# Sums over experts moved to DRAM, and two sets of second-matrix operands, in an attention and mixture kernel

## The chip, the cores and the metric

The kernel runs on one core of a Trainium2 chip. The metric is the device time of one execution in microseconds (us). TensorE (PE in the profile) multiplies matrices, VectorE (DVE) and ScalarE (ACT) do the elementwise work, and SyncE (SP) issues nearly all DMA transfers, in the order of its instruction stream. Each engine executes its own stream in order and waits on semaphores for the others.

## The reference, cut to what matters

Linear attention feeds a dense network with 2048 hidden features, and its output feeds a mixture of eight experts whose weights come from a balanced table P. All products and sums are float32 in the reference.

```python
N, D, E, F = (2304, 512, 8, 1024)
...
P = np.exp(logits)
for _ in range(8):
    P /= P.sum(1, keepdims=True) + 1e-09
    P /= P.sum(0, keepdims=True) + 1e-09
    P *= N / E
out = np.zeros((N, D), dtype=np.float32)
for e in range(E):
    h = np.maximum(x @ w1[e], 0.0)
    ye = h @ w2[e]
    out += P[:, e:e + 1] * ye
```

## The kernel before

The dense network is treated as two layers `e` = 0 and 1 (`M` = 2), the experts as `e` = 2 to 9 (`NL` = 10). The 2304 rows are 18 tiles of 128, and they are worked in three parts `p` of six tiles. Each float32 operand is stored as a pair of float16 numbers (`halves`, line 379: one ACT cast and one DVE subtraction), and each product is three float16 matmuls (`hi_lo_mms`, line 390). The products of an expert use a scheme of seven instead of eight half-size products; the index `m_` runs over these seven.

For each expert and part there are four units of the class `Quad` (line 1068: first matrix, 7 x 6 matmuls of 384 columns each, results split into the hidden operands `hop`) and then three units of the class `Outs` (line 1250: second matrix, 7 x 4 x 3 matmuls of 256 columns each). So an expert has 12 Quads with 504 matmuls of 384 columns, and 9 Outs with 756 of 256 columns. At most three units are in flight (`flight`, line 1003), four have buffers (`unit_bufs`), and eight banks of PSUM are shared (`banks`). A unit gives its place in `flight` back in `give`, after its products `c21` and `c12` have been read out of PSUM. Of an Outs, `take` (line 1296) reads `c11`, `c12` or `c22` out of PSUM with one DVE addition, hands the bank on in `after`, and only then calls `add_to`, which adds the scaled block to the sum over experts. `take_c21` calls `add_to` on the PSUM block itself and hands the bank on after it.

The sums over experts, `acc` (line 988), are 18 tiles of 2 KB a partition in SBUF at the region `BR`. They stay there from the first expert to the last; the attention and the dense network used the region before (`ys`, line 407). An Outs changes two tiles, in four blocks of 256 columns.

The weights of an expert come in four parts of 1 MB (`st_load`, line 853): parts 0 and 1 are the first matrix, parts 2 and 3 the second. They pass through three staging slots of 8 KB a partition (`st_view`, line 839), in the order of the number `4 * e + part`; a part is loaded when the part three numbers earlier has been consumed (`st_guard`, line 843). DVE takes the largest absolute value of a part (`st_max`, line 868), `w_prep` (line 883) makes a scale from both parts of a matrix, and `w1_split` (line 918) and `w2_split` (line 958) scale the part and write the float16 pairs into `W1` and `W2`. There is one set of each. A product's operand of expert `e` is written after the last matmul of expert `e - 1` on it (`w1_used`, `w2_used`). So the first matrix is split while the last part's Outs of the expert before run, and the second while the first part's Quads of its own expert run. With three slots, part 3 of an expert takes the slot of its part 0, and so is loaded only when half of that expert's first matrix has been split.

The order of all instructions on each engine is written by a planner (`Sched`, line 96): a list scheduler with estimated costs, run several times, that takes what can start first and, of that, what is due first by the latest starts of the run before. DMA issues are planned on SP the same way, with a cost by size (`dma`, line 336). The inputs of a part, `X`, are 2.7 MB and come back from DRAM by `x_load` (line 746) for most parts.

## Time and profile before

| | |
|---|---|
| median of 3 runs | 1834.15 us (1829.84 to 1835.17) |
| time of the profiled execution | 1839.03 us |
| its span, first to last instruction | 1837.2 us |
| mean granted TensorE clock | 0.986 |
| PE / PEld busy | 97% / 70% |
| DVE / ACT busy | 83% / 59% |
| DMA traffic | 129.09 MB, 70 GB/s |

Busy shares are over the span. "Idle before" in the groups names what ended an engine's wait. A window row gives, for a stretch of the span, each engine's busy time and number of instructions, then the granted clock (1.00 is 2.4 GHz and 0.50 is 1.2 GHz), the mean busy share of the DMA engines and what they moved in GB/s.

### The profile page before, as it was taken

Reading aid. Unit: us, or ns where it says so; the run is one execution under the profiler, and the core shown is the slowest. Engines: PE = TensorE matmul, PEld = TensorE weight load, DVE = VectorE, ACT = ScalarE, POOL = GpSimd, SP = SyncE. Lnnn points to the kernel's source line nnn. Section 1 sums busy time; section 2 is a strip of 40 time slices with the busy share of each in tenths; the row PEclk is TensorE's granted clock in tenths of the full one; section 3 lists DMA queues with packets and bytes.
Section 4 is the critical chain, followed back from the end, with each engine's and each line's share of the span. In section 5 each row is a group of like instructions: output and inputs, shape, how many; then the busy total and the mean of one; then the engine's idle time right before and its main releaser. Section 6 shows DMA issues by size and latency. Waiting matters only on the chain.

```text
span 1837.2 us, 31972 instructions
## 1 busy us (share of the span) xinstructions
PE 1773.4 (97%) x12898; PEld 1277.2 (70%) x12898; DVE 1523.3 (83%) x3294; ACT 1086.8 (59%) x2284; POOL 2.8 (0%) x11
## 2 busy tenths in 40 slices
PE   4989999999999999999999999999999999999999
PEld 3855666666677767776777777677767777776777
DVE  5789976779887999699779869985998799789866
ACT  4757855443676676455656546764576566567543
POOL 0000000000000000000000000000000000000000
PEclk9789999999999999999999999999999999999999
DMA  9523221202021111012101210211121012102121
GB/s 292 184 78 129 70 70 74 94 1 106 1 107 61 47 67 69 33 47 107 61 1 47 106 61 13 95 47 61 47 102 66 1 47 107 61 1 68 51 95 36
DMA packets 37062, 129.09 MB, mean 70 GB/s; under 512 B 5553, under 2 KB 13233, under 8 KB 34225
## 3 DMA queue, kind: packets, MB, share of 16 engines
q1 hardware_dynamic: 34160, 127.02, 19.3%
q8 instruction: 101, 1.65, 0.4%
q10 hardware_dynamic: 2752, 0.03, 0.1%
q14 instruction: 49, 0.39, 0.1%
HBM read 108.55 MB, written 18.48 MB: 69 GB/s over the span
## 4 chain that ended last, share of the span: by engine, by line
PE 82%; DVE 14%; ACT 2%; DMA 1%; ACTq 1%; issue 0%; SPq 0%; DVEq 0%
PE ps L396 78%; DVE arena L162 14%; ACT arena L162 2%; PE ps L522 1%; PE ps L444 1%; PE ps L532 1%; DMA arena<-in_v_dram 1%; PE ps L162 1%; ACTq L1383 0%; SPq L162 0%; DMA arena<-in_qT_dram 0%; PE ps L700 0%; ACT L162 0%; PE ps L492 0%; ACTq L1381 0%
## 5 line engine op out<-in xcount | busy, mean ns | idle before, releaser
L396 PE MATMUL ps<-arena 128*128 128x256 f16 (+1 forms) x12240 | 1688.7, 301 | 30.3 <-DVE arena L162 19.8
L396 PEld LDWEIGHTS <-arena 128*128 128x128 f16 x12240 | 1201.2, 98 | 509.1 <-issue 40.5
L162 ACT ACTIVATE arena<-arena 128x384 f16<-128x384 f32 (+5 forms) x1494 | 792.0, 577 | 250.1 <-DVE arena L162 206.4
L162 DVE TENSOR_TENSOR arena<-arena 128x384 f16<-128x384 f32 (+6 forms) x1592 | 837.2, 570 | 53.4 <-ACT arena L162 50.0
L162 ACT ACTIVATE arena<-ps 128x384 f32<-128x384 f32 (+3 forms) x691 | 305.0, 452 | 427.0 <-PE ps L396 388.9
L162 DVE SCALAR_TENSOR_TENSOR arena<-ps,arena 128x384 f32<-128x384 f32 (+1 forms) x447 | 247.5, 555 | 101.1 <-PE ps L396 92.6
L162 DVE SCALAR_TENSOR_TENSOR arena<-arena 128x384 f32<-128x384 f32 (+3 forms) x526 | 283.9, 550 | 15.4 <-ACT arena L162 11.4
L162 DVE TENSOR_TENSOR arena<-ps,arena 128x256 f32<-128x256 f32 x216 | 89.9, 420 | 102.3 <-ACT arena L162 75.6
L162 DVE TENSOR_REDUCE arena<-arena 128x1 f32<-128x1024 f32 (+5 forms) x130 | 100.0, 771 | 3.2 <-DMA arena<-in_w_dram 2.7
L162 ACT ACTIVATE arena<-ps,arena 128x384 f32<-128x384 f32 x96 | 55.3, 577 | 55.8 <-PE ps L396 52.9
L162 DVE TENSOR_SCALAR arena<-arena 128x1 f32<-128x1 f32 (+8 forms) x212 | 49.3, 246 | 5.5 <-DMA arena<-in_w_in_dram 4.5
L444 PE MATMUL ps<-arena 128*128 128x128 f32 (+1 forms) x160 | 27.7, 323 | 27.1 <-DMA arena<-in_v_dram 27.1
L444 PEld LDWEIGHTS ps<-arena 128*128 128x128 f32 (+1 forms) x160 | 23.3, 215 | 31.2 <-issue 28.2
L522 PE MATMUL ps<-arena 128*128 128x384 f32 (+1 forms) x64 | 27.0, 587 | 2.2 <-DMA arena<-in_qT_dram 2.2
L162 DVE TENSOR_SCALAR_CACHE_REDUCE arena<-arena 128x512 f32<-128x512 f32 x32 | 21.5, 673 | 7.8 <-ACT arena L162 7.8
L532 PEld LDWEIGHTS ps<-arena 128*128 128x128 f32 x144 | 21.5, 229 | 2.0 <-issue 1.7
L522 PEld LDWEIGHTS ps<-arena 128*128 128x128 f32 x64 | 16.6, 281 | 7.0 <-issue 2.5
L532 PE MATMUL ps<-arena 128*128 128x2 f32 x144 | 20.5, 272 | 0.0
L162 DVE TENSOR_REDUCE arena<-ps 128x1 f32<-128x128 f32 x26 | 7.3, 283 | 13.3 <-PE ps L162 13.3
L162 PE MATMUL ps<-arena 128*128 128x128 f32 (+2 forms) x92 | 17.8, 280 | 0.4 <-ACT arena L162 0.4
L162 DVE TENSOR_TENSOR arena<-arena,ps 128x384 f32<-128x384 f32 x24 | 11.9, 548 | 2.1 <-PE ps L162 2.0
L162 PEld LDWEIGHTS ps<-arena 128*128 128x128 f32 x68 | 11.1, 190 | 1.7 <-issue 0.3
(22 smaller groups left out, 37.0 us busy)
## 6 DMA issues: line engine op xcount, KB each, us to landing
arena<-xd SPq DMA_DIRECT2D x16, 2688.0 KB, 9.5
arena<-in_w_dram SPq DMA_DIRECT2D x64, 512.0 KB, 3.6
xd<-arena SPq DMA_DIRECT2D x5, 2688.0 KB, 8.4
arena<-in_w_in_dram SPq DMA_DIRECT2D x16, 512.0 KB, 5.0
arena<-in_w_out_dram SPq DMA_DIRECT2D x16, 512.0 KB, 4.2
arena<-in_qT_dram SPq DMA_DIRECT2D x6, 768.0 KB, 11.4
out_dram<-arena SPq DMA_DIRECT2D x36, 128.0 KB, 1.7
arena<-in_k_dram SPq DMA_DIRECT2D x4, 1024.0 KB, 10.3
```

The lines of the kernel that those rows point to most:

```text
L162: way[2](*way[3], **way[4])
L396: r = nc.tensor.matmul(ps[:, 0:ncols], x, y, start=(start and i == 0 and m == 0), stop=(stop and i == n - 1 and m == 2), skip_group_check= ...
L444: nc.tensor.matmul(ps[:, sl], kt[0:n, c, sl], vt[0:n, c, sl], start=(c == 0), stop=(c == 4))
L522: nc.tensor.matmul(ps[:, r0:r1], kvbd[b][:, c, :], qs[j][:, c, r0:r1], start=True, stop=True)
L532: nc.tensor.matmul(sums[:, o * H + 2 * c:o * H + 2 * c + 2], sq[:, o * P:(o + 1) * P], heads, start=True, stop=True)
```

## The change

Three things are changed, and the arithmetic is the same.

- The sums move to a DRAM tensor `accd` of 9 blocks of 128 x 1024 float32 (512 KB, one block for an Outs). In SBUF stay two slots of 4 KB a partition. For each Outs in order, `acc_load` waits until the Outs two earlier has left its slot and, from the second expert on, until the block of the expert before has been stored, and loads it; the first expert's Outs write to an empty slot. After the last of its four additions an Outs stores its block (512 KB), except those of the last expert, which write the result as before. `add_to`, and all writes of the first expert, wait for the slot (`acc_ready`).
- The region `BR` that the sums leave holds a second set of `W2`. Even and odd experts use different sets, and an operand is written after the last use two experts earlier. The first write to the second set waits for the end of the work on the network's output (`x_done`).
- From the third expert on (`e` > `M + 1`) the weights are loaded in the order second matrix, first matrix (`pos`). `make_pcol` waits for both scales.

Hunks that only rename `st_view(4 * e + part)` to `st_view(e, part)` and `st_free[4 * e + part]` to `st_free[pos(e, part)]` are left out.

```diff
@@ -296,6 +296,7 @@
     arena = pool.tile([P, SIZE_ALL // 4], F32, tag="arena", name="arena")
     bank_tiles = [psp.tile([P, 512], F32, tag=f"ps{i}", name=f"ps{i}") for i in range(8)]
     xd = dram.tile([NP, P, 7 * 4 * NB], F16, tag="xd", name="xd")
+    accd = dram.tile([NP * TPB, P, 2 * D], F32, tag="accd", name="accd")
 
     def program(sc):
         ev = sc.event
...
@@ -813,6 +814,8 @@
         def make_pcol(e):
 
             yield pm_done
+            for which in range(2):
+                yield scale_done[e][which]
             if e >= M + 2:
                 yield acc_done[e - 2]
             f = small()
@@ -836,9 +839,13 @@
         acc_done = [ev(NTILE * 2) for _ in range(NL)]
         raws_done = ev(2)
 
-        def st_view(n):
-            off = STR + n % 3 * 8192
-            return view(off, F32, 2, F) if n % 4 < 2 else view(off, F32, 2, 2, D)
+        def pos(e, part):
+
+            return 4 * e + (part if e <= M + 1 else (part + 2) % 4)
+
+        def st_view(e, part):
+            off = STR + pos(e, part) % 3 * 8192
+            return view(off, F32, 2, F) if part < 2 else view(off, F32, 2, 2, D)
 
         def st_guard(n):
             guards = [st_free[n - 3]] if n >= 3 else []
@@ -851,10 +858,9 @@
             return guards
 
         def st_load(e, part):
-            n = 4 * e + part
-            for g in st_guard(n):
+            for g in st_guard(pos(e, part)):
                 yield g
-            st = st_view(n)
+            st = st_view(e, part)
             if part < 2:
                 src = w1[e - M].rearrange("(a c p) f -> p c a f", a=2, c=2)[:, part]
             else:
@@ -869,16 +875,23 @@
             yield st_done[e][part]
             if e > M:
                 yield wmax_read[2 * (e - 1) + part // 2]
-            x = flat(st_view(4 * e + part))
+            x = flat(st_view(e, part))
             for i in range(2):
                 yield V(1024, nc.vector.tensor_reduce, wam[part // 2][:, (part % 2) * 2 + i:(part % 2) * 2 + i + 1],
                         x[:, i * 1024:(i + 1) * 1024], op=amax, axis=AX.X, apply_absolute_value=True)
             wmax[2 * e + part // 2].set()
 
         W1 = view(W1R, F16, 7, 2, 2 * 512).rearrange("p m a (c f) -> p m a c f", c=2)
-        W2 = view(W2R, F16, 7, 2, 4 * 256).rearrange("p m a (i d) -> p m a i d", i=4)
+
+        W2 = [[view(o + 4096 * i, F16, 2, 4, 256) for i in range(7)] for o in (W2R, BR)]
         W2N = view(W2R, F16, 8, 2, D)
         USED = (0, 4, 1, 5, 6, 3, 2)
+
+        def w2_guards(e, m_):
+
+            if e == M:
+                return w2_used[e - 1][2 * m_:2 * m_ + 2] if m_ < 4 else []
+            return x_done if e == M + 1 else [w2_used[e - 2][m_]]
 
         def w_prep(e, which):
 
...
@@ -953,20 +966,18 @@
                             yield q_used[q]
                     yield from split(W2N[:, f, 0, :], W2N[:, f, 1, :], st[:, i, kk], s[:, f:f + 1])
                     w2_done[e][f].set()
-            st_free[4 * e + 2 + h].set()
+            st_free[pos(e, 2 + h)].set()
 
         def w2_split(e, h, s):
 
-            st = st_view(4 * e + 2 + h)
+            st = st_view(e, 2 + h)
             b11, b12, b21, b22 = st[:, :, 0, 0:256], st[:, :, 0, 256:512], st[:, :, 1, 0:256], st[:, :, 1, 256:512]
 
             def put(m_, x):
-                if e > M:
-                    yield w2_used[e - 1][m_]
-                elif m_ < 4:
-                    yield w2_used[e - 1][2 * m_]
-                    yield w2_used[e - 1][2 * m_ + 1]
-                yield from halves(W2[:, m_, 0, 2 * h:2 * h + 2, :], W2[:, m_, 1, 2 * h:2 * h + 2, :], x)
+                for g in w2_guards(e, m_):
+                    yield g
+                w = W2[(e - M) % 2][m_]
+                yield from halves(w[:, 0, 2 * h:2 * h + 2, :], w[:, 1, 2 * h:2 * h + 2, :], x)
                 w2_done[e][m_][h].set()
 
             for i in range(2):
@@ -982,10 +993,23 @@
             yield tt(512, b21, b21, b11, sub)
             yield from put(3, b21)
             yield from put(2, b22)
-            st_free[4 * e + 2 + h].set()
-
-
-        acc = [view(BR + t * 2048, F32, D) for t in range(NTILE)]
+            st_free[pos(e, 2 + h)].set()
+
+
+
+        acc = [view(BR + 28672 + i * 4096, F32, 2, D) for i in range(2)]
+        outs = [(e, p, o) for e, p in order if e >= M for o in range(TPB)]
+        acc_ready, acc_left = [{k_: ev() for k_ in outs} for _ in range(2)]
+
+        def acc_load(n):
+            e, p, o = outs[n]
+            if n >= 2:
+                yield acc_left[outs[n - 2]]
+            if e > M:
+                yield acc_left[e - 1, p, o]
+                yield from dma(P * D * 8, (acc[n % 2], accd[p * TPB + o].rearrange("p (b d) -> p b d", b=2)))
+            acc_ready[e, p, o].set()
+
         hops = [view(HR + i * 1536, F16, 2, NB) for i in range(28)]
         hop, hop_free = {}, {}
         unit_bufs = Slots(sc, [])
@@ -1252,16 +1276,16 @@
 
             def __init__(self, n, turn, raw, e, p, o):
                 super().__init__(n, turn, raw)
-                self.e, self.p, self.o, self.left = e, p, o, 3
-                self.ts = [(2 * p + b) * TPB + o for b in range(2)]
+                self.e, self.p, self.o, self.left, self.adds = e, p, o, 3, 4
+                self.ts, self.sums = [(2 * p + b) * TPB + o for b in range(2)], acc[outs.index((e, p, o)) % 2]
 
             def mm(self, ps, m_, start):
-                sl = slice(self.o * P, (self.o + 1) * P)
+                sl, w2 = slice(self.o * P, (self.o + 1) * P), W2[(self.e - M) % 2]
                 for i in range(4):
                     yield from self.ready(m_, i)
                     yield T(mm_cost(3, 256), hi_lo_mms, ps,
                             [(*[hop[(self.e, self.p), m_, i][:, a, sl] for a in range(2)],
-                              W2[:, m_, 0, i, :], W2[:, m_, 1, i, :])],
+                              w2[m_][:, 0, i, :], w2[m_][:, 1, i, :])],
                             256, start and i == 0, i == 3, not start)
                     hop_used[(self.e, self.p), m_, i].set()
                 if self.p == last_p[self.e]:
@@ -1274,19 +1298,31 @@
             def add_to(self, b, d, x):
 
                 e, t = self.e, self.ts[b]
-                dst = acc[t][:, d * 256:(d + 1) * 256]
+                dst = self.acc(b, d)
                 yield pcol_done[e]
+                yield acc_ready[e, self.p, self.o]
                 if e == M + 1:
                     yield pcol_done[M]
                     yield V2(256, nc.vector.tensor_scalar, dst, dst, pcols[M % 3][:, t:t + 1], None, op0=mult)
                 yield V(256, nc.vector.scalar_tensor_tensor, out=dst, in0=x, scalar=pcols[e % 3][:, t:t + 1], in1=dst,
                         op0=mult, op1=add)
 
+            def acc(self, b, d):
+                return self.sums[:, b, d * 256:(d + 1) * 256]
+
             def end(self, b, d):
                 acc_done[self.e].set()
+                self.adds -= 1
                 if self.e == NL - 1:
                     t, sl = self.ts[b], slice(d * 256, (d + 1) * 256)
-                    sc.add(dma(P * D * 2, (out[t * P:(t + 1) * P, sl], acc[t][:, sl])))
+                    sc.add(self.store(P * D * 2, out[t * P:(t + 1) * P, sl], self.acc(b, d)))
+                elif self.adds == 0:
+                    sc.add(self.store(P * D * 8, accd[self.p * TPB + self.o].rearrange("p (b d) -> p b d", b=2), self.sums))
+
+            def store(self, nbytes, dst, src):
+                yield from dma(nbytes, (dst, src))
+                if self.adds == 0:
+                    acc_left[self.e, self.p, self.o].set()
 
             def release(self):
                 self.left -= 1
@@ -1297,7 +1333,8 @@
 
                 x = self.buf[n][:, 0:256]
                 if self.e == M:
-                    x = acc[self.ts[b]][:, d * 256:(d + 1) * 256]
+                    x = self.acc(b, d)
+                    yield acc_ready[self.e, self.p, self.o]
                 yield V(256, nc.vector.tensor_tensor, x, ps[:, 0:256], self.buf[n][:, 0:256], op=add)
                 after()
                 if self.e > M:
@@ -1317,7 +1354,8 @@
 
             def take_c21(self, ps):
                 if self.e == M:
-                    yield A(256, nc.scalar.activation, acc[self.ts[1]][:, 0:256], ps[:, 0:256], AF.Copy)
+                    yield acc_ready[self.e, self.p, self.o]
+                    yield A(256, nc.scalar.activation, self.acc(1, 0), ps[:, 0:256], AF.Copy)
                 else:
                     yield from self.add_to(1, 0, ps[:, 0:256])
                 self.give(ps)
@@ -1430,10 +1468,12 @@
             sc.add(make_x(p), LAGS["make_x"])
         for n, (e, p) in enumerate(order):
             sc.add(x_load(e, p, n), -1.0)
+        for n in range(len(outs)):
+            sc.add(acc_load(n), -1.0)
         sc.add(sinkhorn(), -0.4)
         for e in range(NL):
             if e >= M:
-                for part in range(4):
+                for part in sorted(range(4), key=lambda x: pos(e, x)):
                     sc.add(st_load(e, part), 0.01 * part)
                     sc.add(st_max(e, part), LAGS["max"])
             for which in range(2):
```

## Rows read from the trace of the kernel before

**Rows 1.** The page: busy time of two engines, and the chain that ended last.
```profile
PE 1773.4 (97%) x12898; PEld 1277.2 (70%) x12898; DVE 1523.3 (83%) x3294; ACT 1086.8 (59%) x2284; POOL 2.8 (0%) x11
PE 82%; DVE 14%; ACT 2%; DMA 1%; ACTq 1%; issue 0%; SPq 0%; DVEq 0%
```

**Rows 2.** Windows: one expert, and six experts from middle part to middle part.
```profile
879.10:1048.30 169.20, 166.04 (x1261) 124.05 (x1259) 142.44 (x293) 102.55 (x219) 0.00 (x0) 0.99 0.16 58
706.50:1727.70 1021.20, 1000.35 (x7583) 746.19 (x7583) 860.06 (x1788) 611.65 (x1310) 0.00 (x0) 0.99 0.16 56
```

**Rows 3.** Windows: calm stretches, matmuls of 384 columns, then of 256 columns.
```profile
360.00:405.00 45.00, 45.00 (x280) 27.27 (x278) 30.45 (x61) 15.86 (x30) 0.00 (x0) 1.00 0.00 1
957.90:980.70 22.80, 22.80 (x211) 20.43 (x209) 22.80 (x48) 12.64 (x27) 0.00 (x0) 1.00 0.14 42
```

**Rows 4.** Windows: two of the six changes of expert.
```profile
835.00:860.00 25.00, 20.89 (x150) 15.73 (x148) 24.12 (x48) 15.04 (x35) 0.00 (x0) 0.86 0.29 111
1005.00:1030.00 25.00, 21.84 (x163) 16.65 (x162) 24.42 (x49) 16.26 (x38) 0.00 (x0) 0.93 0.29 112
```

**Rows 5.** Timeline of PE, then a window, at the first of those changes.
```profile
847.22 8.99 PE L396 MATMUL ps<-arena 128*128 128x256 f16 x54 [3.10 <-DVE arena L162]
...
847.20:853.20 6.00, 5.98 (x29) 4.09 (x29) 6.00 (x12) 3.40 (x7) 0.00 (x0) 0.50 0.14 57
```

**Rows 6.** Groups of DVE by shape, 985 to 1035 us: the weights' work.
```profile
L162 DVE TENSOR_TENSOR arena<-arena 128x512 f16<-128x512 f32 x14 | 9.4, 687 | 0.6 <-ACT arena L162 0.6
L162 DVE TENSOR_TENSOR arena<-arena 128x512 f32<-128x512 f32 x8 | 5.5, 684 | 0.0
L162 DVE TENSOR_REDUCE arena<-arena 128x1 f32<-128x1024 f32 x4 | 4.8, 1211 | 0.0
```

**Rows 7.** Windows: Outs of a middle part, then of the last part.
```profile
902.00:930.00 28.00, 28.00 (x245) 23.80 (x244) 13.26 (x31) 8.58 (x20) 0.00 (x0) 1.00 0.26 100
957.00:985.00 28.00, 28.00 (x247) 23.96 (x246) 27.74 (x57) 14.68 (x32) 0.00 (x0) 1.00 0.24 72
```

**Rows 8.** Timeline of SP: loads of weights during a last part's Outs.
```profile
974.50 8.48 SPq L162 DMA_DIRECT2D arena<-in_w_dram  x4
```

**Rows 9.** The page's DMA issues (KB each, median us to landing), then in_w_dram's landing.
```profile
arena<-xd SPq DMA_DIRECT2D x16, 2688.0 KB, 9.5
arena<-in_w_dram SPq DMA_DIRECT2D x64, 512.0 KB, 3.6
xd<-arena SPq DMA_DIRECT2D x5, 2688.0 KB, 8.4
...
out_dram<-arena SPq DMA_DIRECT2D x36, 128.0 KB, 1.7
...
DMA to landing us min/median/max: 3.2/3.6/5.4
```

**Rows 10.** Timeline of DVE, additions to the sums in a middle part's Outs.
```profile
917.21 0.48 DVE L162 SCALAR_TENSOR_TENSOR arena<-arena 128x256 f32<-128x256 f32 x1
...
925.78 0.48 DVE L162 SCALAR_TENSOR_TENSOR arena<-arena 128x256 f32<-128x256 f32 x1
...
933.58 0.48 DVE L162 SCALAR_TENSOR_TENSOR arena<-ps,arena 128x256 f32<-128x256 f32 x1
```

**Rows 11.** The same in a last part's Outs.
```profile
979.42 1.27 DVE L162 SCALAR_TENSOR_TENSOR arena<-arena 128x256 f32<-128x256 f32 x3
...
986.27 0.48 DVE L162 SCALAR_TENSOR_TENSOR arena<-ps,arena 128x256 f32<-128x256 f32 x1 [0.31 <-PE ps L396]
```

**Rows 12.** Second expert's first Outs: window, and DVE's timeline of its additions.
```profile
660.00:710.00 50.00, 44.78 (x354) 34.44 (x353) 49.70 (x125) 30.27 (x64) 0.00 (x0) 1.00 0.27 98
...
704.90 0.48 DVE L162 SCALAR_TENSOR_TENSOR arena<-ps,arena 128x256 f32<-128x256 f32 x1
...
706.10 0.48 DVE L162 SCALAR_TENSOR_TENSOR arena<-arena 128x256 f32<-128x256 f32 x1
```

**Rows 13.** Waits of the SP queue over the whole span: us in total, times, longest.
```profile
SPq L162 <- DVE arena L162: 1172.6, 104, 71.1
```

More of the change, by code (lines that the diff above doesn't have):

```diff
@@ L605, in st_chunk @@
         def st_chunk(e, part, i, turn=None):
-            st, slots = st_view(4 * e + part), raw_slots[(0, 0, 1, 1, 2, 2, 3, 4)[4 * e + part]]
+            st, slots = st_view(e, part), raw_slots[(0, 0, 1, 1, 2, 2, 3, 4)[4 * e + part]]
             h = i // 2, i % 2
@@ L918, in w1_split @@
         def w1_split(e, c, s):
-            st = st_view(4 * e + c)
+            st = st_view(e, c)
             a11, a21, a12, a22 = st[:, 0, 0:512], st[:, 0, 512:1024], st[:, 1, 0:512], st[:, 1, 512:1024]
@@ L940, in w1_split @@
             yield from put(2, a12)
-            st_free[4 * e + c].set()
+            st_free[pos(e, c)].set()
         def w2_halves(e, h, s):
-            st = st_view(4 * e + 2 + h)
+            st = st_view(e, 2 + h)
             for kk in range(2):
@@ L955, in w2_halves @@
                     w2_done[e][f].set()
-            st_free[4 * e + 2 + h].set()
+            st_free[pos(e, 2 + h)].set()
         def w2_split(e, h, s):
-            st = st_view(4 * e + 2 + h)
+            st = st_view(e, 2 + h)
             b11, b12, b21, b22 = st[:, :, 0, 0:256], st[:, :, 0, 256:512], st[:, :, 1, 0:256], st[:, :, 1, 256:512]
             def put(m_, x):
-                if e > M:
-                    yield w2_used[e - 1][m_]
-                elif m_ < 4:
-                    yield w2_used[e - 1][2 * m_]
-                    yield w2_used[e - 1][2 * m_ + 1]
-                yield from halves(W2[:, m_, 0, 2 * h:2 * h + 2, :], W2[:, m_, 1, 2 * h:2 * h + 2, :], x)
+                for g in w2_guards(e, m_):
+                    yield g
+                w = W2[(e - M) % 2][m_]
+                yield from halves(w[:, 0, 2 * h:2 * h + 2, :], w[:, 1, 2 * h:2 * h + 2, :], x)
                 w2_done[e][m_][h].set()
```

## Prediction, made before the changed kernel ran

> **What bounds the kernel now.** I read the page first: PE is busy 97% of the span and is 82% of the chain that ended last, DVE 14% of it [rows 1]. A busy PE need not be one that advances, so the next question is how long an expert takes against what its matmuls need. In a calm stretch of the dense network 280 matmuls of 384 columns take 45.0 us, 160.7 ns each; in a calm stretch of Outs 211 of 256 columns take 22.8 us, 108 ns each [rows 3]. An expert's 504 and 756 would so need 504 x 0.1607 + 756 x 0.108 = 81.0 + 81.6 = 162.6 us, and with the four small matmuls of its two scales about 163.4. The six experts between 706.5 and 1727.7 us took 1021.2 us, 170.2 each [rows 2]: 40.8 us more than six times 163.4. That is the room.
>
> Where is it lost? Over these 1021.2 us PE is idle for 1021.2 - 1000.35 = 20.85 us [rows 2]. The windows at the changes of expert show where: 25 us long, they hold 4.1 and 3.2 us of idle PE, and at the other four it is 3.1 to 3.8. At 835 to 860 the granted clock is 0.86 and at 1005 to 1030 it is 0.93 [rows 4]; two more changes (1175 and 1350) show 0.93 and the last two 1.00. After 3.10 us of waiting for DVE the clock is 0.50, the 1.2 GHz level, for the 6 us that follow [rows 5]. In time this is 25 x 0.14 + 3 x 25 x 0.07 = 8.75 us. Idle and clock together make 20.85 + 8.75 = 29.6 us, and the remaining 11 of the 40.8 are small gaps that I do not assign.
>
> What PE waits for is DVE, which is busy 24.1 and 24.4 of 25 us there [rows 4], though over six experts it has 860 of 1021 us, 84% [rows 2]. The fifty microseconds from 985 hold 22 DVE operations of 512 columns [rows 6]; Quads and Outs have 384 or 256, so these are `w2_split` (2 halves of 7 subtractions and 4 differences), 14.9 us, and 4 maxima, 4.8 us. They fall among the Quads whose results the same engine must split, and PE's next Outs need both. Their place follows from the code: part 3 gets its staging slot only when `w1_split` has consumed part 0, and its load is issued at 974.5 us, just ahead of the change [rows 8].
>
> **The change, part by part.** The profiled execution took 1839.03 us, 1837.2 of them the span; the median of the runs is 1834.15, so 4.9 us lower. I sum against 1839.03 and take the result off the median.
>
> *Second set of W2, loaded first, for the six changes into the third to the last expert.* Part 2 and 3 of expert e now ask for slots that are free at the change into e - 1, and their operands for a set that was last used in e - 2. The 14.9 + 4.8 us of DVE work can run anywhere in an expert's 163 us. The cover is the Outs of the first two parts: there DVE is busy 13.3 of 28 us [rows 7], so 14.7 us are free, twice an expert. ACT has 8.6 of 28 there and takes its share (the scalings and 14 casts) as well. If that cover were gone, the stall would be back, 29.6 / 6 = 4.9 us a change. What is late next is `w1_split`, which stays between the last Quad of e - 1 and the first of e: there DVE is busy 27.7 of 28 us [rows 7], yet PE has 28.0 of 28.0 in the same window, so it is in time today, and the maxima of the second matrix leave its neighbourhood. I let 90% of 29.6 go: **-27** us (bounds -40.8, if the small gaps go too, and 0).
>
> *The change into the second expert.* Its parts keep the old order, and the DVE is busy 49.7 of 50 us around it [rows 12], with P's table among it. The 5.2 us of idle PE stay: 0.
>
> *The ring.* Each middle Outs adds a load and a store. 63 loads and 63 stores of 512 KB are 66 MB more, on 129. No row shows a store of 512 KB. Its nearest rows are 1.7 us for 128 KB and 8.4 for 2688 KB, which put it at 1.7 + 384 / 2560 x 6.7 = 2.7 us; a load of 512 KB takes 3.6, from 3.2 to 5.4 [rows 9]. A slot's turn is then 2.7 + 3.6 + 0.7 for two issues = 7.0 us. The loads for a part's first two Outs have the 27 us of Quads ahead of them; it is the third that needs the slot of the first. In a middle part the first Outs ends at 917.7 us and the third begins its additions at 925.8, 8.1 us later, and its addition out of PSUM is at 933.6, 15.9 later [rows 10]. That fits. In a last part the delayed c12 of the first ends at 979.9, and the third's addition out of PSUM comes at 986.3, 6.4 us later [rows 11]: 0.6 us short. An addition behind `take` that waits holds no bank, one out of PSUM does; and behind either on DVE stand the rest of `w1_split` and the next Quads' reads of PSUM. So I charge 0.6 us in each of the seven last parts: **+4** us. Nothing in the change can make it a gain. Above, two times the longest load and the issues, 11.5 us, is 5.1 us late in each: 36 us.
>
> Here the trace shows a store's 1.7 us with little beside it, while at 974.5 us four weight loads go out together [rows 8, 9]. By the Trainium skill (DMA: Bandwidth & Descriptors, section "Latency and other measured facts") an access to HBM takes 0.2 us on average and 2 us under high load, and this is most of a transfer's fixed cost. If each store and load beside those weights paid that difference, an estimate from that page is 3.6 us more for a turn in the seven last parts, 25 us in all, and 1839 us instead of 1814; it is a way into the first rival below. The DMA share in that window is 0.24 [rows 7], and I do not take that as high load.
>
> *The second expert's start.* The scaled table is late, and the additions of its first part come in a burst: the first Outs ends at 706.6 us, and the third's read of PSUM stands at 704.9, before it [rows 12]. With the ring it follows at 706.6 + 7.0 = 713.6, 8.7 us later, and holds one of three places in flight. The two others are Quads of 6.7 us each (42 x 0.1607), 13.5 us of PE work. **+3** us, bounds 0 and 9.
>
> *SP and the DVE count.* 126 more issues of about 0.33 us are 42 us on a queue that waits for DVE alone for 1172.6 us [rows 13]: 0. A store waits for the last addition of its Outs, and the next weight loads and `x_load` stand behind it; `x_load` goes out when the part's Quads end, before the first store, and has the 27 us of Outs to land in 9.5 [rows 9]: 0, and up to 1 us in each of 21 parts if a load stands behind a late store. Additions and reads stay as many as they were: 0.
>
> Sum: -27 + 4 + 3 = -20 us. The profiled execution would be 1839.0 - 20 = 1819, the median 1834 - 20 = **1814 us**.
>
> **The rivals.**
>
> *The ring decides (slower).* A turn of 11.5 instead of 7.0 us costs 36 us in the last parts: 1834 - 27 + 36 + 3 = 1846. It decides when a turn is so long that seven last parts lose the 24 us that the rest brings, 3.4 us each, so from a turn of 6.4 + 3.4 = 9.8 us. For it: the planner orders DVE by an estimated DMA time, and DVE executes in order, so a late load stops what could have run. Against it: 8.1 and 15.9 us in middle parts, and loads that have a median of 3.6.
>
> *Half of the stall stays.* DVE is full from the last Outs of one expert on, and what remains behind is `w1_split`'s backlog, paid by the first Quads' splits. Then 13 of 27 us go: 1834 - 13 + 7 = 1828. For it: 27.7 of 28 us. Against it: PE at 28.0 in that window.
>
> *The work is not moved.* The planner gives the second matrix's split no early turn, or its loads wait behind others on SP, and only the ring is added: 1834 + 7 = 1841. Against it: it takes whatever can start first, and DVE has the gaps.
>
> **How the numbers follow.** The forecast has 0.68, and its own range is 1799 to 1826; the ring 0.13; half of the stall 0.13; not moved 0.06. A difference under 0.3%, 5.5 us, cannot be told from none. The range of 8 in 10 takes the forecast and the half stall, with some of its cost: 1799 to 1836. Faster is the forecast and half of the second rival, 0.75; same the other half and a little of the third, 0.09; slower the rest, 0.16.
>
> **What would show it.** The windows of six experts should fall from 170.2 to about 166 each, with no 1.2 GHz stretch after 840 us, and DVE's operations of 512 columns should show two groups an expert, one among middle Outs. PE's waits for DVE at the changes should be under 1 us. DVE waiting for DMA of `accd` at third Outs is the ring's price: under 1 us each by the forecast, 3 or more by the rival. The prediction is wrong if PE waits there, if a 512 KB store takes over 5 us, or if the changes of expert still hold 3 us of idle PE.

## The result, and the profile after

The changed kernel takes 1814.8 us (median of 4 runs, 1813.68 to 1820.52), against 1834.7 for the kernel before: a ratio of 0.9902, with a 95% interval of 0.9874 to 0.993. A second comparison on another occasion gave 1815.9 and a ratio of 0.9877 (0.9863 to 0.9892). The forecast was 1814.

The page of the changed kernel, rows of parts 1, 4 and 6 (the last: KB each, median us from issue to landing). DVE has 9% of the chain instead of 14% [rows 1], and the transfers of the sums are there, on 195 MB in all:

```profile
PE 1760.7 (97%) x12898; PEld 1270.2 (70%) x12898; DVE 1517.4 (84%) x3292; ACT 1085.9 (60%) x2286; POOL 2.8 (0%) x11
...
PE 85%; DVE 9%; DMA 2%; ACT 2%; ACTq 1%; SPq 0%; issue 0%; DVEq 0%
...
arena<-in_w_dram SPq DMA_DIRECT2D x64, 512.0 KB, 4.7
accd<-arena SPq DMA_DIRECT2D x63, 512.0 KB, 3.0
arena<-accd SPq DMA_DIRECT2D x63, 512.0 KB, 3.7
```

To see where the time went, I count matmuls. All 6192 of 384 and 6048 of 256 columns are in each trace, so the same number marks the same place of the work. A step below runs from the first 256-column matmul of an expert's second part (its number is 756 per expert before it, plus 253) to the same of the next expert. The profiled executions differ by 25.4 us in span:

| stretch of the work | before | after | difference |
|---|---|---|---|
| start to the first matmul of the network | 102.2 | 95.8 | -6.4 |
| from there to the first matmul of an Outs | 392.3 | 393.1 | +0.8 |
| first expert, to its second part | 57.1 | 59.6 | +2.5 |
| step into the second expert | 175.3 | 182.0 | +6.7 |
| step into the third | 172.6 | 165.4 | -7.2 |
| steps into the fourth to the eighth, five | 848.6 | 827.0 | -21.6 |
| from there to the last matmul | 84.9 | 84.9 | 0 |

Windows over the last six of these steps, of the kernel before and then of the changed one (us, busy time and instructions of PE, PEld, DVE, ACT and POOL, granted clock, DMA share, GB/s):

```profile
727.00:1748.20 1021.20, 1000.35 (x7584) 746.20 (x7583) 859.28 (x1784) 611.39 (x1311) 0.00 (x0) 0.99 0.16 57
```

```profile
730.40:1722.80 992.40, 990.29 (x7585) 742.48 (x7583) 849.65 (x1778) 607.69 (x1305) 0.00 (x0) 1.00 0.32 115
```

PE's idle time in them falls from 20.85 to 2.1 us, and the low-clock stretches are gone (1.00). With the 8.75 us that the prediction put on the low clock, that is 20.85 - 2.11 + 8.75 = 27.5 of the 28.8 us.

The changed kernel was profiled a second time ("after, again" below). There the same six steps took 995.5 us, so the difference is 25.7 us: the step into the third expert is 168.7 instead of 165.4 us. All other stretches of the two profiles agree within 0.3 us. So a difference of about 3 us in that one step says nothing by itself.

The changes of expert look different from [rows 4] and yet alike. These are windows of the changed kernel at the same two changes, counted from the same matmuls (the first moved by +3 us, the second by -4), and DVE's groups over the same fifty microseconds as [rows 6]:

```profile
838.00:863.00 25.00, 24.57 (x212) 20.50 (x211) 25.00 (x54) 18.72 (x37) 0.00 (x0) 1.00 0.36 136
1001.00:1026.00 25.00, 25.00 (x208) 20.13 (x207) 25.00 (x52) 18.34 (x41) 0.00 (x0) 1.00 0.29 111
```

```profile
L162 DVE TENSOR_TENSOR arena<-arena 128x512 f16<-128x512 f32 x14 | 9.4, 688 | 0.0
...
L162 DVE TENSOR_TENSOR arena<-arena 128x512 f32<-128x512 f32 x8 | 5.4, 685 | 0.0
```

DVE is as full as before (25.0 of 25 us in both), and the same 14 and 8 operations of a second matrix stand in the same place. But PE has 24.6 and 25.0 of 25, where it had 20.9 and 21.8. By the order of the slots these operations make operands of the next expert, not of this one: the staging slot that `w1_split` frees first at this change takes the last part of the next expert's second matrix. Nothing here waits for them, so the Quads' results can go ahead of them.

### The profile page after: what moved, and what is told of

Read it like the earlier page. It is cut to its first block, busy times and chain, and to the rows that moved or that the text cites. A ratio compares the mean times of both kernels' runs of the same rounds, so it can differ in the third digit from the quotient of the medians.

```text
span 1811.8 us, 32211 instructions
## 1 busy us (share of the span) xinstructions
PE 1760.7 (97%) x12898; PEld 1270.2 (70%) x12898; DVE 1517.4 (84%) x3292; ACT 1085.9 (60%) x2286; POOL 2.8 (0%) x11
## 4 chain that ended last, share of the span: by engine, by line
PE 85%; DVE 9%; DMA 2%; ACT 2%; ACTq 1%; SPq 0%; issue 0%; DVEq 0%
PE ps L397 81%; DVE arena L162 9%; ACT arena L162 2%; PE ps L445 1%; PE ps L523 1%; DMA arena<-in_v_dram 1%; PE ps L533 1%; DMA accd<-arena 1%; PE ps L162 1%; DMA arena<-accd 0%; ACTq L1421 0%; SPq L162 0%; DMA arena<-in_qT_dram 0%; PE ps L701 0%; ACT L162 0%
## 5 line engine op out<-in xcount | busy, mean ns | idle before, releaser
L397 PE MATMUL ps<-arena 128*128 128x384 f16 (+1 forms) x12240 | 1682.6, 300 | 17.4 <-ACT arena L162 15.7
L162 ACT ACTIVATE arena<-arena 128x384 f16<-128x384 f32 (+4 forms) x1496 | 795.7, 578 | 240.1 <-DVE arena L162 200.0
L162 DVE TENSOR_TENSOR arena<-arena 128x384 f16<-128x384 f32 (+5 forms) x1592 | 844.1, 575 | 45.0 <-ACT arena L162 40.7
L445 PE MATMUL ps<-arena 128*128 128x128 f32 (+1 forms) x160 | 28.8, 331 | 27.5 <-DMA arena<-in_v_dram 27.5
L162 DVE TENSOR_SCALAR arena<-arena 128x1 int32<-128x1 int32 (+8 forms) x210 | 49.4, 249 | 5.5 <-DMA arena<-in_w_in_dram 4.5
L162 DVE TENSOR_SCALAR_CACHE_REDUCE arena<-arena 128x512 f32<-128x512 f32 x32 | 21.6, 689 | 7.9 <-ACT arena L162 7.9
L523 PE MATMUL ps<-arena 128*128 128x384 f32 (+1 forms) x64 | 21.2, 482 | 0.8 <-DMA arena<-in_qT_dram 0.8
L533 PEld LDWEIGHTS ps<-arena 128*128 128x128 f32 x144 | 18.4, 199 | 2.8 <-ACT arena L162 1.4
L523 PEld LDWEIGHTS ps<-arena 128*128 128x128 f32 x64 | 13.3, 230 | 5.0 <-issue 1.5
L162 DVE TENSOR_TENSOR arena<-arena,ps 128x384 f32<-128x384 f32 x24 | 11.9, 551 | 2.6 <-PE ps L162 2.6
L162 PEld LDWEIGHTS ps<-arena 128*128 128x128 f32 x68 | 11.2, 190 | 1.9 <-issue 0.3
```

The source lines that it names most:

```text
L162: way[2](*way[3], **way[4])
L397: r = nc.tensor.matmul(ps[:, 0:ncols], x, y, start=(start and i == 0 and m == 0), stop=(stop and i == n - 1 and m == 2), skip_group_check= ...
L445: nc.tensor.matmul(ps[:, sl], kt[0:n, c, sl], vt[0:n, c, sl], start=(c == 0), stop=(c == 4))
L523: nc.tensor.matmul(ps[:, r0:r1], kvbd[b][:, c, :], qs[j][:, c, r0:r1], start=True, stop=True)
L533: nc.tensor.matmul(sums[:, o * H + 2 * c:o * H + 2 * c + 2], sq[:, o * P:(o + 1) * P], heads, start=True, stop=True)
```

## The experiments

Every ratio is to runs of the kernel before on the same chip. The steps of all profiled executions, in us as in the table above ("2 + 3" is the sum of the steps into the second and third expert, "five" the later ones):

| kernel | time, ratio (95%) | start | first expert | into 2nd | into 3rd | 2 + 3 | five |
|---|---|---|---|---|---|---|---|
| before | 1 | 102.2 | 57.1 | 175.3 | 172.6 | 347.9 | 848.6 |
| after | 0.9902 (0.9874 to 0.993) | 95.8 | 59.6 | 182.0 | 165.4 | 347.4 | 827.0 |
| ring only | 1.0063 (1.0038 to 1.0088) | 102.8 | 58.9 | 172.7 | 175.5 | 348.2 | 854.2 |
| old order | 1.0045 (1.0028 to 1.0063) | 98.2 | 59.0 | 172.7 | 175.8 | 348.5 | 854.5 |
| no traffic | 0.9892 (0.986 to 0.9925) | 95.5 | 58.1 | 178.0 | 165.1 | 343.1 | 828.3 |
| load twice | 0.9928 (0.9905 to 0.9952) | 102.5 | 60.6 | 176.9 | 168.0 | 344.9 | 829.1 |
| one set | 1.0845 (1.0799 to 1.089) | 99.6 | 58.9 | 177.1 | 196.1 | 373.2 | 970.5 |
| second too | 0.9944 (0.9923 to 0.9965) | 98.6 | 59.6 | 184.7 | 167.6 | 352.3 | 826.0 |
| extra slot | 0.9891 (0.9853 to 0.9929) | 102.5 | 59.5 | 177.5 | 169.1 | 346.6 | 826.3 |
| both | 0.993 (0.9903 to 0.9958) | 98.5 | 59.6 | 185.0 | 167.3 | 352.3 | 826.0 |
| after, again | 0.9877 (0.9863 to 0.9892) | 96.1 | 59.6 | 182.3 | 168.7 | 351.0 | 826.8 |
| hold | 0.989 (0.9873 to 0.9906) | 97.9 | 59.6 | 178.1 | 172.8 | 350.9 | 827.5 |
| hold, slot | 0.9883 (0.9868 to 0.9897) | 98.2 | 59.5 | 177.5 | 168.5 | 346.0 | 827.0 |
| hold late, slot | 0.9903 (0.9886 to 0.992) | 98.6 | 59.6 | 172.4 | 180.4 | 352.8 | 825.2 |

**The ring alone.** One set of W2 and the old order, so that the sums' way through DRAM is all that is left of the change.

```diff
-        W2 = [[view(o + 4096 * i, F16, 2, 4, 256) for i in range(7)] for o in (W2R, BR)]
+        W2 = [[view(o + 4096 * i, F16, 2, 4, 256) for i in range(7)] for o in (W2R, W2R)]
...
-            return x_done if e == M + 1 else [w2_used[e - 2][m_]]
+            return [w2_used[e - 1][m_]]
...
-            return 4 * e + (part if e <= M + 1 else (part + 2) % 4)
+            return 4 * e + part
```

> The sums pass through DRAM and the two slots, as changed; the second matrix's operands have one set again, written after the last use in the expert before, and all parts are loaded in the old order. Theory (the gain is the second matrix's work leaving the change of expert, the ring costs about 6 us, nearly all at the second expert's start): the stalls at the six changes come back in full, about 20 us of idle PE, and the time is 1835 + 6 = 1841 us, 1836 to 1846. Rival (the ring has a price in each of 21 parts, 1 us or more of PE, that the second set outweighs in the changed kernel): 1856 us or more, with PE idle at third Outs in middle parts too.

1846.8 us, 11 more than before, between the two expectations. The stalls of before are back, and the five steps have 5.6 us more than before. These are the waits of PE from 735 us on, in the kernel before and then in this one (us, times, longest):

```profile
PE ps L396 <- DVE arena L162: 15.9, 12, 3.1
PE ps L396 <- ACT arena L162: 5.4, 7, 1.4
```

```profile
PE ps L397 <- DVE arena L162: 22.4, 14, 2.8
PE ps L397 <- ACT arena L162: 6.9, 11, 1.7
```

They rise from 21.3 to 29.3 us. All but one of them, of 0.47 us, stand 105 to 132 us into a step, which is the change of expert, and none at a middle part's third Outs, as the rival had it. So the kernel with the ring loses more where the changes of expert are already late. Whether that is the traffic, or the order that the planner wrote around it, isn't shown: no kernel has the slots without the traffic in the old order.

**The second set and the ring, in the old order.**

```diff
-            return 4 * e + (part if e <= M + 1 else (part + 2) % 4)
+            return 4 * e + part
```

> The changed kernel, but all experts load their parts in the old order, first matrix then second; the second set and the ring stay. Theory A (the order is needed: the second matrix's last part can't be loaded before half of the first matrix of the same expert is split, so its split stays at the change of expert although a free set waits for it): PE is idle about 3 us at each change, 1830 to 1842 us. Theory B (the free set is what matters): within 5 us of the changed kernel, 1810 to 1820 us.

1843.1 us: theory A, 1 us above its range. The free set changes nothing by itself (854.5 us in five steps against the ring's 854.2). By the order of the slots its last part still can't be loaded before the change of expert: the four loads go out from 968 us on, where the kernel before has them from 974.5 us on [rows 8]. Waits of PE from 735 us on:

```profile
PE ps L397 <- DVE arena L162: 20.0, 12, 2.8
PE ps L397 <- ACT arena L162: 8.3, 11, 1.7
```

**The new order with one set.** The first two lines of the first diff, applied to the changed kernel.

> The changed kernel with one set of the second matrix's operands: the ring and the new order of the parts stay, an operand is written after the last use in the expert before. Theory (order and set are worth something only together): worse than either alone, since the second matrix's parts then hold their staging slots until the last Outs of the expert before, and the first matrix's second part, which needs one of these slots, comes later still; a split of about 10 us, a load of 4.7, maxima of 2.4 and a split of 12 in a row are some 25 us of idle PE at each of six changes, about 1815 + 150 = 1965 us. Rival (the early load and the early maxima are the gain, the free set is not needed): 1815 to 1825 us.

1990.5 us, 25 more than the theory had it. The order without the second set is worse than nothing: the second matrix's parts sit in two of three staging slots until the last Outs of the expert before, and the first matrix's second part waits behind them. PE is idle 23 to 28 us in each of the six steps. PE's timeline at one change (start us, us, what, idle before):

```profile
1013.51 2.12 PE L397 MATMUL ps<-arena 128*128 128x256 f16 x18 [0.38 <-DVE arena L162]
1029.25 0.79 PE L162 MATMUL ps<-arena 128*128 128x128 f32 x2 [13.61 <-DVE arena L162]
```

The two small matmuls belong to the scale of the late part; PE waits 13.6 us for DVE's maxima of it. So neither piece gains without the other.

**The ring's traffic taken away.** This kernel leaves out that the sums are carried from expert to expert.

```diff
-                yield from dma(P * D * 8, (acc[n % 2], accd[p * TPB + o].rearrange("p (b d) -> p b d", b=2)))
...
-                    sc.add(self.store(P * D * 8, accd[self.p * TPB + self.o].rearrange("p (b d) -> p b d", b=2), self.sums))
+                    acc_left[self.e, self.p, self.o].set()
```

> The changed kernel without the 63 loads and 63 stores of the sums: the two slots are handed on as soon as the four additions are done, and each expert adds to what its slot holds. Left out: the sums are not carried from expert to expert. Theory (the ring costs only at the second expert's start, where PE is idle 4.8 us and then runs at 1.2 GHz for 3.4 us): 1815 - 6.5 = 1808 us, 1804 to 1812. Rival (the ring's waits and its 66 MB are paid in small pieces in all parts): 1800 us or less.

1813.5 us, within the interval of the changed kernel and 1.5 above the theory's range. In the five steps nothing is gained (828.3 against 827.0): with the second matrix out of the way, the loads and stores cost nothing to be seen there. Of the 6.5 us that I had expected at the second expert's start, that step is 4.0 shorter, and the first expert 1.5. The stretch of the network is 2.4 us longer in this profile (395.5 instead of 393.1), so the time does not follow by as much.

**Each load done twice.** The line of `acc_load` that issues the load stands twice.

> The changed kernel with each load of a block of sums done twice, one after the other into the same slot, so that a slot's turn is about 3.0 + 2 x 3.7 + 1.1 = 11.5 us instead of 7.5. Price of the prediction (what the third Outs of a last part is late is paid one for one): 4 us in seven parts, 28 us, 1843 us, with PE idle there. Rival (the additions of the first Outs are ordered earlier and the four unit buffers cover the rest, so only the second expert's start pays, about 4 us more): 1815 to 1823 us, DVE waiting for DMA of accd in sum three times the 11 us of the changed kernel.

1821.2 us: the time of that run's rival, but not for its reasons. The price of the prediction, 28 us in last parts, isn't paid; the five steps have 829.1 us. But the step into the second expert, which the rival had pay about 4 us, is 5.1 us shorter than in the changed kernel. As it is also 4.0 shorter without the traffic, that step does not measure the ring: the planner writes another order there for each kernel. Of the 10.7 us that this profile is longer, 6.7 lie before the network and 3.4 in the network, where no sums are moved. And DVE's wait for the sums does not triple. Here it is in the changed kernel and in this one, from 735 us on:

```profile
DVE arena L162 <- DMA arena<-accd: 11.1, 8, 3.2
```

```profile
DVE arena L162 <- DMA arena<-accd: 18.0, 13, 3.3
```

SP's timeline in a middle and a last part of the changed kernel shows the turn of a slot, from the store of the first Outs to the load for the third:

```profile
916.90 0.32 SPq L162 DMA_DIRECT2D accd<-arena  x1
920.24 0.32 SPq L162 DMA_DIRECT2D arena<-accd  x1
...
973.40 0.32 SPq L162 DMA_DIRECT2D accd<-arena  x1
973.81 1.27 SPq L162 DMA_DIRECT2D arena<-in_w_dram  x2
976.49 0.34 SPq L162 DMA_DIRECT2D arena<-accd  x1
```

The loads go out 3.3 and 3.1 us after the stores, and these two land 3.5 and 4.5 us later: turns of 6.8 and 7.6 us, against the 7.0 of the prediction. Over the second to the seventh expert the median turn is 6.8 us in middle parts, 7.7 in last and 10.3 in first parts. What changed is the room for it. DVE's timeline in that last part, the last addition of the first Outs and the third's addition out of PSUM:

```profile
972.89 0.48 DVE L162 SCALAR_TENSOR_TENSOR arena<-arena 128x256 f32<-128x256 f32 x1
...
985.44 0.48 DVE L162 SCALAR_TENSOR_TENSOR arena<-ps,arena 128x256 f32<-128x256 f32 x1
```

From 973.4 to 985.4 are 12.1 us, not 6.4 [rows 11]: the planner, which knows of the ring, wrote DVE's order anew, and the first Outs's late addition stands earlier in it. In the six last parts from the second expert on, the time from the store to that addition is 9.3 to 12.8 us and longer than the turn in each. With each load done twice the turns there grow to a median of 13.2 us, and the planner leaves 11.9 to 15.6.

**What is left, at the second expert.** PE's timeline of the changed kernel at the two long waits that remain:

```profile
670.69 1.65 PE L397 MATMUL ps<-arena 128*128 128x256 f16 x7 [4.35 <-ACT arena L162]
...
725.82 2.49 PE L397 MATMUL ps<-arena 128*128 128x384 f16 x9 [4.77 <-ACT arena L162]
```

The first I took for the old stall (the second expert keeps the old order), the second for the third Outs that holds a unit buffer until its block is loaded. Three kernels try to take these away: the new order from the second expert on; a third slot for that one Outs, in an operand of W2 that is empty then; and both.

```diff
-            return 4 * e + (part if e <= M + 1 else (part + 2) % 4)
+            return 4 * e + (part if e <= M else (part + 2) % 4)
```

```diff
-        acc = [view(BR + 28672 + i * 4096, F32, 2, D) for i in range(2)]
+        acc = [view(o, F32, 2, D) for o in (BR + 28672, BR + 32768, W2R + 6 * 4096)]
...
+        THIRD = NP * TPB + 2
+        acc_slot = [2 if n == THIRD else (n - (n > THIRD)) % 2 for n in range(len(outs))]
...
+            third = [acc_left[outs[NP * TPB + 2]]] if e == M + 2 and m_ == 6 else []
+            return x_done if e == M + 1 else [w2_used[e - 2][m_]] + third
```

> The changed kernel with the new order of parts also for the second expert (condition e <= M in pos). Theory (the 5 us of idle PE at the second expert's first Outs are the same stall, with its second matrix's split in the old place): they go, with the 1.2 GHz stretch behind them, 1815 - 7 = 1808 us. Rival (DVE is full there anyway, by the balancing of P's table and the network's output, and the work only stalls something earlier): 1812 to 1820 us.

> The changed kernel with a third slot for one Outs alone, the third of the second expert's first part, in the operand 6 of the first set of W2, which is empty between the first expert's last Outs and the third expert's split. Theory (the 4.8 us of idle PE at 720 us and the 3.4 us at 1.2 GHz behind them are that Outs holding one of four unit buffers until its block is loaded): they go, 1815 - 6 = 1809 us. Rival (the burst of additions after the late table is itself the bound): 1813 to 1817 us.

> Both: the new order for the second expert too, and the third slot for its third Outs. If both theories hold: 1815 - 13 = 1802 us. If both rivals hold: 1812 to 1820 us.

1824.3, 1817.8 and 1822.4 us: on the rivals' side, and all three above even the rivals' ranges, the second by 0.8 us. Windows from 550 to 735 us, of the changed kernel and then of the one with the order for the second expert too:

```profile
550.00:735.00 185.00, 175.12 (x1367) 130.86 (x1366) 168.69 (x407) 122.32 (x263) 0.00 (x0) 0.97 0.24 89
```

```profile
550.00:735.00 185.00, 174.00 (x1348) 127.34 (x1347) 173.94 (x416) 125.01 (x267) 0.00 (x0) 0.98 0.27 98
```

DVE goes from 168.7 to 173.9 of 185 us. PE goes from 1367 to 1348 matmuls, but this kernel is also 3.7 us further behind when the window begins. With the third slot the wait at 720 us is gone and the step into the second expert is 4.5 us shorter (177.5). The step into the third is 169.1 us, as in the second profile of the changed kernel (168.7), and the time is the same; this profile's start is 6.7 us longer. So what the slot gains is less than these times can show.

The wait at 720 us is not the ring's alone either. PE waits there for only 1.2 us with each load done twice, and for only 0.6 us with two slots and the first hold of the next paragraph:

```profile
734.55 4.40 PE L397 MATMUL ps<-arena 128*128 128x384 f16 x33 [1.20 <-ACT arena L162]
```

```profile
726.48 4.40 PE L397 MATMUL ps<-arena 128*128 128x384 f16 x33 [0.58 <-ACT arena L162]
```

The last idea was that the third expert's second matrix now does its work too early, in this full stretch. It was held until P's table was done; the same with the third slot; and held until the third Outs had stored.

```diff
             yield st_done[e][part]
+            if e == M + 2 and part > 1:
+                yield pm_done
```

> The changed kernel once more, to stand beside the next three on the same chip: 1815 us, and once more 161 to 167 us for each of the six experts from the third to the fourth and on, 180 or more for the second expert's step (its first part's end to the next expert's first part's end).

> The changed kernel, but the third expert's second matrix is not touched (maxima, scale, split) before P's table is done; its loads stay early. Theory (the second expert's step grew from 175 to 182 us because the third expert's second matrix now runs its 20 us of DVE work in the stretch where DVE has no free time): the step falls to 175 to 177 us, the six later ones stay at 165 to 166, 1815 - 6 = 1809 us. Rival (the ring alone made it longer): 1813 to 1817 us.

> The same hold, and the third slot for the second expert's third Outs. If the ring and the early work share the 6.7 us, the step falls to 173 us and the time to 1806; if the hold alone explains it, as the kernel with the hold; if neither, 1813 to 1817 us.

> As the last, but the third expert's second matrix is held until the second expert's third Outs has stored its sums, about 10 us after the table. If the burst of additions after the table is what the early split disturbs: 1 to 3 us less than the kernel with hold and slot, about 1804 us. If not: the same within 2 us, or more, as the work then has less time.

1815.9, 1818.4, 1816.7 and 1821.1 us: no hold brings the 1804 to 1809 us that its theory had. The hold does shorten the step into the second expert, from 182 to 178 and, held longest, to 172.4 us. But the step into the third grows, to 172.8 and 180.4 from 165.4 and 168.7, and with the first hold the sum of the two is the repeat's (350.9 and 351.0). In the longest hold PE waits in one piece for DVE's maxima (its waits from 550 to 900 us):

```profile
PE ps L162 <- DVE arena L162: 6.8, 1, 6.8
```

Over these kernels, except the one with one set, the two steps together stay between 343 and 353 us, and before has 347.9. None of the versions is faster than the changed kernel beyond its interval.

## Why the prediction was right, and where it was not

**The number.** Forecast -20, measured -19.9, and -23.4 in the second comparison. The time is right, and the mechanism of its largest term too; the terms were not. That it fits to 0.1 us is luck. Without the stretch before the network's first matmul, the two profiles of the changed kernel are 19.0 and 15.4 us shorter than that of the kernel before. In the first, 28.8 us won in the six steps stand against 6.7 lost in the step before them and 2.5 in the first expert, for neither of which the forecast had the right reason.

**The six changes, -27.** The six steps lost 28.8 us, of which 27.5 are idle time and clock, under the ceiling of 29.6; in the second profile they lost 25.7. Set and order are needed together, as two kernels with one of them show. But the first of the six is not a gain: its -7.2 (-3.9 in the second profile) stands beside the +6.7 of the step before it. The third expert's second matrix left its own change and went to the stretch of [rows 12], where DVE had 49.7 of 50 us already. Kernels that hold it back only move the stall between the two steps. What is won is the -21.6 of the five later steps. That DVE's amount of work bounds these two steps is likely from its 168.7 of 185 us, but only the order was varied, so it isn't shown.

**The cover.** I let the work run in the free 14.7 us of middle Outs [rows 7], and expected a group of 512-column operations there. It is wrong: the fifty microseconds from 985 have the same 22 operations as [rows 6]. It is the due time that moved, by an expert, not the place. The price came out right because a full DVE (25.0 of 25 us) did not stop PE while what filled it could wait.

**The change into the second expert, 0.** It was the step that failed. It keeps its old order, as I said, but it was priced alone, with nothing arriving in it; the third expert's work did, as the holds show.

**The ring, +4 and +3.** The turn of 7.0 us was right for middle parts (6.8) and a little short for last parts (7.7). The +4 in last parts was oversized: without the traffic the five steps have 828.3 us, with it 827.0. The gap of 6.4 us that I took from [rows 11] was not fixed; it is 12.1 in the changed kernel's order. For the second expert's third Outs, PE does wait 4.77 us at 720 us and runs at the low clock after it (0.72 over the next 6.2 us):

```profile
725.80:732.00 6.20, 6.18 (x32) 3.72 (x32) 6.08 (x13) 3.28 (x8) 0.00 (x0) 0.72 0.00 0
```

But as the order there is another in each kernel, the +3 is neither confirmed nor refuted. Not foreseen was the first expert: its third Outs writes PSUM's results into the slot that the first must have stored. It takes 57.1 us before, 58.1 without the traffic and 58.9 to 60.6 in the kernels with it. In the ring-only kernel the five steps are 5.6 us longer than before; where the stall is gone, nothing of this is seen.

The prediction put nothing on first parts, and there the ring reaches PE for more than 0.4 us once. Ten of the 63 stores take 5.3 to 9.4 us, although their median is 3.0; over 5 us was a sign that the prediction gave of being wrong. One of them stands in the third expert's first part. Rows of the changed kernel's second profile show what follows from it: SP's two stores and the loads behind them, the time to landing of the first store, DVE's wait for the load at an addition out of PSUM, PE's wait for DVE, and the window after that:

```profile
867.17 3.27 SPq L162 DMA_DIRECT2D accd<-arena  x2
...
875.94 1.54 SPq L162 DMA_DIRECT2D arena<-accd  x2
...
DMA to landing us min/median/max: 8.8/8.8/8.8
...
879.49 0.95 DVE L162 SCALAR_TENSOR_TENSOR arena<-ps,arena 128x256 f32<-128x256 f32 x2 [1.44 <-DMA arena<-accd]
...
880.49 3.79 PE L397 MATMUL ps<-arena 128*128 128x384 f16 x12 [1.47 <-DVE arena L162]
...
880.60:884.00 3.40, 3.40 (x12) 1.66 (x11) 2.85 (x8) 1.59 (x4) 0.00 (x0) 0.50 1.00 377
```

The wait of 1.47 us and the 1.7 us lost in 3.4 us at half the clock are most of the 3.3 us by which the step into the third expert differs between the two profiles. In the first, the same load came 1.50 us late for DVE, PE waited 0.39 us and the clock stayed up. It is the way that the prediction described, an addition out of PSUM that waits and holds a bank, but in a part that it did not charge. DVE's longest wait for a load, 3.2 us, is also in a first part:

```profile
1205.51 0.48 DVE L162 SCALAR_TENSOR_TENSOR arena<-ps,arena 128x256 f32<-128x256 f32 x1 [3.20 <-DMA arena<-accd]
```

That is the size that the prediction gave to its first rival, but PE waited only 0.34 us behind it.

**The start.** 6.4 of the profile's 25.4 us lie before the network's first matmul, where the change does nothing by itself. Windows of the first 110 us, before and after:

```profile
0.00:110.00 110.00, 80.70 (x410) 65.00 (x411) 71.86 (x201) 65.17 (x133) 2.77 (x11) 0.84 0.69 231
```

```profile
0.00:110.00 110.00, 80.46 (x462) 63.65 (x462) 77.91 (x221) 70.47 (x147) 2.78 (x11) 0.92 0.70 231
```

PE is busy as long and gets further (462 matmuls instead of 410), at a granted clock of 0.92 instead of 0.84. The other profiles say how much of the 6.4 us is the change's. The kernel before, the ring-only and the old-order kernel run the same sequence of operations, by type and shape, on PE, DVE and ACT up to 516 us, and reach the network's first matmul at 102.2, 102.8 and 98.2 us. The changed kernel, its repeat and the first and last hold have one sequence up to 640 us, and reach it at 95.8, 96.1, 97.9 and 98.6. So one and the same order varies by up to 4.6 us from execution to execution, and that much of the 6.4 cannot be put down to the change. Whether the rest belongs to the planner's new order stays open.

**Transfers under load.** A load of weights takes 4.7 us in the median instead of 3.6 [rows 9], and in the kernel without the traffic 3.8:

```profile
arena<-in_w_dram SPq DMA_DIRECT2D x64, 512.0 KB, 3.8
```

So the added traffic makes these transfers slower, by about 1 us. The Trainium skill (DMA: Bandwidth & Descriptors, section "Latency and other measured facts") gives an access to HBM 0.2 us on average and 2 us at high load. The trace agrees in direction. The 512 KB store has a median of 3.0 us and its load 3.7, and the turn in last parts 7.7, so the 3.6 us more for a turn there, and the 25 us in all, that the prediction estimated from that page of the Trainium skill were not there.

## What to carry to other kernels

A second set of operands paid here only when its data could also arrive ahead: look at the whole path of an operand, staging slots and their order included, and move all of it by the same amount. A full engine hurts where what it does is due; moving the due time can be enough, without any idle time to move the work into. And when work is taken out of a place, ask which place it arrives in: here 7.2 of 28.8 us in one profile, and 3.9 of 25.7 in the other, went from one stall to another. Before a few microseconds are put down to a change, look at how far one and the same order varies: here by 4.6 us before the network, and by 3.3 us in one step.

## What was not expected of the hardware

66 MB more went through DRAM, at a DMA share of 0.32 instead of 0.16 over six experts. Its cost was not to be seen in the five later steps: 827.0 us with it and 828.3 without. Even with each load done twice, at median turns of 10 us in middle and 13 to 14 us in other parts, five steps took 829.1. The medians hide a long tail: stores of one size landed in 2.6 to 9.4 us, median 3.0.
